# Reordering the first window's second product of an mLSTM cell with a GELU block: who copies columns, when weights are converted, and what a load queues behind

## The chip, the cores and the metric

The kernel runs on one core of a Trainium2 chip. The metric is the device time of one execution in microseconds (us). The program uses five engines, each with an instruction stream of its own: TensorE (PE in the profile; its weight loads are shown apart as PEld), VectorE (DVE), ScalarE (ACT), GpSimd (POOL) and SyncE (SP), which in this kernel issues every DMA transfer. [...] The kernel is written under a manual schedule: on each engine the instructions run in the order in which the program emits them, so moving a call in the source moves its instructions in the stream of each engine it uses.

## The reference

An mLSTM cell (4 batches, 8 heads, 768 steps, head size 40) feeds a two-layer block (3072 tokens, 320 to 2048 to 320) with the quick GELU between.

```python
for t in range(S):                                  # per batch and head
    m_new = max(f[t] + m, i[t])
    C = exp(f[t] + m - m_new) * C + exp(i[t] - m_new) * outer(v[t], k[t])
    n = exp(f[t] + m - m_new) * n + exp(i[t] - m_new) * k[t]
    y[t] = sigmoid(o[t]) * (C @ q[t]) / max(abs(n @ q[t]), 1)
    m = m_new
x = y as (3072, 320)
h = x @ w_in                                        # the first product
out = (h * sigmoid(1.702 * h)) @ w_out              # the second product
```

## The kernel before

The 768 steps are cut into six windows of 128 (w = 0 to 5). Inside a window the recurrence is written as a masked attention (scores, weights, values) plus a term from the carried state. Each window then goes through the first product (`up`, TensorE, with a GELU on ScalarE) and the second (`down` in window 0, `down_fast`, a form with fewer multiplications, in the others). While TensorE does the second product of window w, the attention of window w+1 is slipped in between its blocks. Window 0 is special in two ways: its attention stands ahead of everything, and the 20 pieces of the two weight matrices arrive as 64-bit numbers in this window and are turned into fp32 by ScalarE and VectorE (`convert`), just ahead of the blocks that use them.

Loads. Every one goes out on SP, in program order. `load_blocks` brings k and q of the next window in 32-column blocks, in 32 small transfers, so that VectorE can transpose them (`transposes`); the buffers `k_bl` and `q_bl` exist once. `fetch` brings one piece of weights; pieces 10 to 15 take the six buffers of one pool, and pieces 16 to 19 take them over when the pieces before have been converted.

```python
    def load_blocks(w, which=slice(0, 2)):
        both = (k_bl, k), (q_bl, q)
        for dst, src in both[which] if isinstance(which, slice) else both[which:which + 1]:
            for two in range(2):
                for d in range(0, D, 32):
                    n = min(32, D - d)
                    r = two * 64 + d
                    for g in range(L // 32):
                        t = w * L + g * 32
                        nc.sync.dma_start(
                            out=dst[r:r + 32, :, g, 0:n],
                            in_=src[:, two:H:2, t:t + 32, d:d + n].rearrange("b j s d -> s (b j) d"))
...
    def fetch(n):
        pool = gp if 6 <= n < 10 else sp
        bits[n] = pool.tile([128, 512, 2], U32, tag="g", name="bits")
        for r, c, src in pieces[n][1]:
            dst = bits[n][r, c].rearrange("p a two -> p (a two)")
            if len(src.shape) == 3:
                dst = dst.rearrange("p (j m) -> p j m", j=src.shape[1])
            nc.sync.dma_start(out=dst, in_=src)
...
    def convert(n, engines="AV"):
        lo, hi, dst = bits[n][:, :, 0], bits[n][:, :, 1], pieces[n][0]
        dst_u = dst.bitcast(U32)
        if "A" in engines:
            A.activation(out=dst, in_=hi.bitcast(FP), func=AF.Abs)
            A.activation(out=lo, in_=lo, func=AF.Copy, scale=2.0 ** -29)
        if "V" not in engines:
            return
        V.tensor_scalar(out=dst, in0=dst, scalar1=HI_MIN, scalar2=HI_MAX, op0=OP.max, op1=OP.min)
        V.tensor_scalar(out=dst_u, in0=dst_u, scalar1=3, scalar2=0x3FFFFFFF, op0=OP.logical_shift_left,
                        op1=OP.bitwise_and)
        V.scalar_tensor_tensor(out=dst_u, in0=hi, scalar=0xC0000000, in1=dst_u, op0=OP.bitwise_and,
                               op1=OP.bitwise_or)
        V.tensor_tensor(out=dst_u, in0=dst_u, in1=lo, op=OP.add)
```

The columns of the gates (a transpose on TensorE, evicted to `cols`), the weights of later windows (an exponential for each of 8 heads, then a causal mask on GpSimd), and the first lines of scores and values:

```python
        c = cols[w] = gate.tile([L, 3 * BH + BH // 2], FP, name="cols")
        V.tensor_copy(out=c[:, 0:BH], in_=pt[:, 0:BH])
        A.activation(out=c[:, BH:3 * BH], in_=pt[:, BH:3 * BH], func=AF.Exp, scale=-1.0)
        if w in dec:
            A.activation(out=c[:, 3 * BH:n], in_=pt[:, 3 * BH:n], func=AF.Exp)
...
    def weights(w, b):                    # the branch of w > 0
            x = wt[w, b].rearrange("s p i t -> s (p i) t")
            for h in range(H):
                A.activation(out=x[:, h, :], in_=x[:, h, :], func=AF.Exp, scale=-1.0,
                             bias=cols[w][:, b * H + h:b * H + h + 1])
        x = wt[w, b].rearrange("s p i t -> s (p i) t")
        G.affine_select(out=x, in_=x, compare_op=OP.is_ge, fill=0.0, base=0, pattern=[[0, H], [1, L]],
                        channel_multiplier=-1)
        if w and b == 0:
            A.activation(out=eo[w], in_=eo[w], func=AF.Tanh, scale=0.5)


        pw = [ps_a.tile([L, NP, L], FP, tag="a", name="p_s") for _ in range(2)]
        for p in range(NP):
            for i in range(2):
                r = slice(i * 64, i * 64 + D)
                T.matmul(pw[i][:, p, :], kT[w, b][r, p, :], qT[w, b][r, p, :], start=True, stop=True)
        for i in range(2):
            V.tensor_tensor(out=wt[w, b][:, :, i, :], in0=pw[i], in1=wt[w, b][:, :, i, :], op=OP.mult)


    def values(w, b):
        ...   # 32 matmuls of wt and v_st into p_o, 16 of qT and state into p_i, then 7 operations on DVE that make y
```

The attention of a batch b runs through four stages, each a step after the one before; a step is called after a block of the second product named in `stops`:

```python
    def attention(w):
        steps = [[(columns, w)]]
        for s in range(B + 3):
            step = []
            for lag, f in ((3, seam), (2, values), (1, scores), (0, weights)):
                if 0 <= s - lag < B:
                    step.append((f, w, s - lag))
            steps.append(step)
        return steps
```

The main loop:

```python
    beside = {0: ((5,), range(10, 16)), 1: ((6, 7, 8), ()), 2: ((9, 10, 11), (16, 17)), 3: ((12, 13, 14), (18, 19)),
              4: ((15, 16), ()), 9: ((17,), ()), 12: ((18,), ()), 14: ((19,), ())}

    def weights_in(n):
        done, ahead = beside.get(n, ((), ()))
        for p in done:
            convert(p)
        for p in ahead:
            fetch(p)

    for w in range(NW):
        more = w + 1 < NW
        for j in range(NF // 2):
            if j % 2 == 0:
                if w == 0 and j == 0:
                    up(w, j, (lambda: values(0, 2), lambda: values(0, 3),
                              lambda: (seam(0, 2), seam(0, 3), convert(3), convert(4))))
                    weights_in(0)
                else:
                    if w == 0:
                        weights_in(j // 2)
                    up(w, j)
            if j == 0 and more:
                load(w + 1, "o")
            if w == 0 and j == 0:
                gates(1)
                load_blocks(1, 0)
                spread(1)
            if w == 1 and j == 1:
                weight_sums()
            if more:
                if w and j == 0:
                    gates(w + 1)
                if j == 4:
                    load(w + 1, "v")
                if w and j == 4:
                    spread(w + 1)
                if j == 4:
                    load(w + 1, "k")
                if j < B:
                    carry(w, j)
                if w == 0 and j == 0:
                    G.memset(q_bl, 0.0)
                    load_blocks(1, 1)
                if 4 <= j < 6 if w else j == 7:
                    first = 2 * j - 8 if w else 0
                    transposes(w + 1, first)
                    transposes(w + 1, first + 1)
            if w and j >= 4:
                hidden_sums(w, (j - 4,), False)
                if j % 2:
                    hidden_sums(w, (j - 5, j - 4), True)
        side = attention(w + 1) if more else []
        if w == 0:

            blocks = [(lambda b=b, n=n: down(w, b, n)) for ns in ((0, 1), (2,), (3,)) for b in range(B) for n in ns]
            stops = (0, 1, 4, 7, 9, 11, 13, 15)
        else:
            blocks = down_fast(w, 0) + down_fast(w, 1)
            stops = (0, 1, 2, 4, 6, 8, 10, 12)
        for i, block in enumerate(blocks):
            if w == 0:
                weights_in(4 + i)
                if i in (6, 9):
                    transposes(1, i // 3)
            if w + 2 < NW and i == (0 if w else 9):
                load_gates(w + 2)
                load_blocks(w + 2)
            block()
            if i in stops and side:
                run(side.pop(0))
```

`down(w, b, n)` is 8 matmul instructions over four of the sixteen row groups of w_out (n = 0 to 3); with n = 3 the sum is copied out on VectorE and stored. The 1280 columns of one n are 2.5 pieces of 512: pieces 10 to 14 serve n = 0 and 1, pieces 15 to 17 serve n = 2, and 17 to 19 serve n = 3.

Of the kernel before, what the change touches and what calls it, by code (L numbers as in the profile page):

```python
# [34 lines left out]
def kernel(  # L35
# [14 lines left out]
    BH = B * H  # L50
    DM = H * D
    DFF = moe_w_in.shape[1]
    NW = S // L
# [21 lines left out]
    V, A, G, T = nc.vector, nc.scalar, nc.gpsimd, nc.tensor  # L75
# [20 lines left out]
    def load(w, what, bs=slice(0, B)):  # L96
        hs = slice(bs.start * H, bs.stop * H)
        for c in what:
            if c == "o" and w not in eo:
                eo[w] = ld.tile([L, BH, D], FP, tag="eo", bufs=1, name="eo")  # L100
            dst, src = {"k": (k_st, k), "q": (q_st, q), "v": (v_st, v), "o": (eo.get(w), o_gate)}[c]
            nc.sync.dma_start(out=dst[:, hs, 0:D],
                              in_=src[bs, :, w * L:(w + 1) * L, :].rearrange("b h s d -> s (b h) d"))
# [13 lines that stand above are left out]
# [60 lines left out]
    def keep_busy(n):  # L177
        for _ in range(n):
            T.matmul(p_idle, idle, idle.unsqueeze(1).to_broadcast([128, 4, 128]), start=True, stop=True)
# [35 lines left out]
# [15 lines that stand above are left out]
# [46 lines left out]
    def columns(w):  # L276
        pt = ps_a.tile([L, 3 * BH + BH // 2], FP, tag="a", name="p_cols")
        T.transpose(pt[:, 0:3 * BH], stacked[w], ident[0:3 * BH, 0:3 * BH])
        n = 3 * BH
        if w in dec:  # L280
            n += BH // 2
            T.matmul(pt[:, 3 * BH:n], half.rearrange("p a b -> p (a b)"), dec[w], start=True, stop=True)
        c = cols[w] = gate.tile([L, 3 * BH + BH // 2], FP, name="cols")
        V.tensor_copy(out=c[:, 0:BH], in_=pt[:, 0:BH])
        A.activation(out=c[:, BH:3 * BH], in_=pt[:, BH:3 * BH], func=AF.Exp, scale=-1.0)
        if w in dec:
            A.activation(out=c[:, 3 * BH:n], in_=pt[:, 3 * BH:n], func=AF.Exp)


    def transposes(w, b):  # L290
        for bl, st, dst, name in ((k_bl, k_st, kT, "kT"), (q_bl, q_st, qT, "qT")):
            dst[w, b] = work.tile([128, NP, L], FP, tag=name, bufs=4, name=name)
            if w:
                V.transpose(out=dst[w, b].rearrange("p j t -> p (j t)"),
                            in_=bl[:, b * NP:(b + 1) * NP].rearrange("p j g c -> p (j g c)"))
                continue
            pt = ps_a.tile([128, NP, L], FP, tag="a", name="p_t")
            for p in range(NP):
                h = b * H + 2 * p
                T.transpose(pt[:, p, :], st[:, h:h + 2, :].rearrange("p a b -> p (a b)"), ident)  # L300
            if b == 0:
                keep_busy(1)
            A.copy(out=dst[w, b], in_=pt)

    def spread(w):

        for b in range(B):
            x = wt[w, b] = work.tile([L, NP, 2, L], FP, tag="wt", bufs=4, name="wt")
            nc.sync.dma_start(out=x.rearrange("s p i t -> s (p i) t"),
                              in_=m_row[w][b * H:(b + 1) * H, :].unsqueeze(0).to_broadcast([L, H, L]))  # L310
# [63 lines left out]
    def seam(w, b):  # L374
        if b == 0:
            xT[w] = work.tile([128, 3, B, L], FP, tag="xT", bufs=1, name="xT")
        px = ps_a.tile([128, 3, L], FP, tag="a", name="p_x")
        for c in range(3):
            T.transpose(px[:, c, :], ys[w, b][:, c * 128:(c + 1) * 128], ident)  # L379
        A.copy(out=xT[w][:, :, b, :], in_=px)  # L380
# [162 lines left out]
    def run(calls):  # L543
        for f, *args in calls:
            f(*args)


    def gate_out(b):
# [31 lines left out]
    convert(2)  # L580
    scores(0, 3)
    columns(0)
    gate_out(2)
    gate_out(3)


    beside = {0: ((5,), range(10, 16)), 1: ((6, 7, 8), ()), 2: ((9, 10, 11), (16, 17)), 3: ((12, 13, 14), (18, 19)),
              4: ((15, 16), ()), 9: ((17,), ()), 12: ((18,), ()), 14: ((19,), ())}

    def weights_in(n):  # L590
        done, ahead = beside.get(n, ((), ()))
# [26 lines that stand above are left out]
                if w and j == 0:  # L618
                    gates(w + 1)
                if j == 4:  # L620
                    load(w + 1, "v")
                if w and j == 4:
                    spread(w + 1)
                if j == 4:
                    load(w + 1, "k")
                if j < B:
                    carry(w, j)
                if w == 0 and j == 0:
                    G.memset(q_bl, 0.0)
                    load_blocks(1, 1)  # L630
                if 4 <= j < 6 if w else j == 7:
                    first = 2 * j - 8 if w else 0
                    transposes(w + 1, first)
                    transposes(w + 1, first + 1)
            if w and j >= 4:
                hidden_sums(w, (j - 4,), False)
                if j % 2:
                    hidden_sums(w, (j - 5, j - 4), True)
        side = attention(w + 1) if more else []
        if w == 0:  # L640

            blocks = [(lambda b=b, n=n: down(w, b, n)) for ns in ((0, 1), (2,), (3,)) for b in range(B) for n in ns]
            stops = (0, 1, 4, 7, 9, 11, 13, 15)
        else:
            blocks = down_fast(w, 0) + down_fast(w, 1)
            stops = (0, 1, 2, 4, 6, 8, 10, 12)
        for i, block in enumerate(blocks):
            if w == 0:
                weights_in(4 + i)
                if i in (6, 9):  # L650
                    transposes(1, i // 3)
            if w + 2 < NW and i == (0 if w else 9):
                load_gates(w + 2)
                load_blocks(w + 2)
            block()
            if i in stops and side:
                run(side.pop(0))


# [28 lines left out]
```

## Time and profile before

| | |
|---|---|
| median of 3 runs | 522.97 us (522.74 to 523.1) |
| the profiled execution | span 519.6 us |
| TensorE busy | 507.5 us, 98% |
| VectorE busy | 268.8 us, 52% |
| ScalarE busy | 168.2 us, 32% |
| GpSimd busy | 71.2 us, 14% |
| 16 DMA engines, loads and stores | 44.21 MB, 45.4% of their time |
| window 0: first product | 29 to 68 us |
| window 0: second product, with the attention of window 1 | 68 to 120 us |
| windows 1 to 5 | 120 to 520 us |

The profile gives each engine's busy time, a strip of its business over the span, the chain of work that ended last, groups of instructions, and who waited for whom. L12 is line 12 of the kernel. "SPq L114" is the issuing of a transfer of line 114 on SP. In a list of waits the engine and line that waited stand ahead of the arrow, and what released it stands behind; then come the total in us, the times, and the longest.

### The profile page before, as it was taken

How to read it: one execution, taken by the hardware profiler on the slowest of the kernel's cores; microseconds unless marked ns; L12 is line 12 of the kernel's file. 1: busy time of each engine (PE TensorE's matmuls, PEld its weight loads, DVE VectorE, ACT ScalarE, POOL GpSimd, SP SyncE). 2: the span in 40 equal slices, each digit the busy share in tenths (PEclk: the TensorE clock that was granted, in tenths of full speed). 3: DMA queues.
4: the chain of work that ended last, by engine and by line, in shares of the span. 5: the costliest groups of instructions: out<-in, count | busy, mean ns of one | idle time of the engine just before them, and what ended most of it. 6: DMA issues, size and time to landing. Idle time of an engine off the chain costs nothing.

```text
span 519.6 us, 9543 instructions
## 1 busy us (share of the span) xinstructions
PE 507.5 (98%) x3838; PEld 351.1 (68%) x3838; DVE 268.8 (52%) x603; ACT 168.2 (32%) x367; POOL 71.2 (14%) x104
## 2 busy tenths in 40 slices
PE   7899999999999999999999999999999999999997
PEld 4774366674437998446999444999643899744797
DVE  6779955972774464156444226565227455203511
ACT  5557617502214510321720222630222450032100
POOL 7231001112500212200212200120220021000000
PEclk9999999999999999999999999999999999999999
DMA  9999689166596102596200395500475000000000
GB/s 148 169 315 286 128 169 204 37 75 117 96 194 76 31 1 48 85 212 75 30 26 14 66 253 61 55 28 1 78 175 89 0 28 1 26 0 0 2 26 25
DMA packets 175692, 44.81 MB, mean 86 GB/s; under 512 B 164352, under 2 KB 170528, under 8 KB 175648
## 3 DMA queue, kind: packets, MB, share of 16 engines
q1 hardware_dynamic: 175648, 44.21, 45.4%
q8 instruction: 30, 0.49, 0.4%
q14 instruction: 14, 0.11, 0.1%
HBM read 40.17 MB, written 4.01 MB: 85 GB/s over the span
## 4 chain that ended last, share of the span: by engine, by line
PE 82%; SPq 5%; DVE 4%; ACT 4%; issue 1%; POOL 1%; DMA 1%; DVEq 0%; POOLq 0%
PE p_out L511 30%; PE p_h L417 28%; PE p_h L423 8%; PE p_o L350 5%; SPq L114 4%; PE p_s L339 4%; PE p_out L457 3%; PE p_i L356 2%; PE p_x L379 1%; DMA v_st<-in_v_dram 1%; PE p_c L391 1%; ACT wt L326 1%; ACT bits L221 1%; ACT g L428 1%; ACT w_in_sb L220 0%
## 5 line engine op out<-in xcount | busy, mean ns | idle before, releaser
L417 PE MATMUL p_h<-xT,w_in_sb 128*128 128x512 f32 (+1 forms) x400 | 175.6, 585 | 1.1 <-ACT xT L380 1.1
L417 PEld LDWEIGHTS p_h<-xT,w_in_sb 128*128 128x128 f32 x400 | 72.7, 190 | 90.3 <-issue 86.9
L428 ACT ACTIVATE g<-p_h 128x512 f32<-128x512 f32 x96 | 54.5, 596 | 132.4 <-PE p_h L423 72.3
L511 PE MATMUL p_out<-w_out_sb,g 128*128 128x160 f32 x480 | 71.3, 302 | 0.0
L511 PEld LDWEIGHTS p_out<-w_out_sb,g 128*128 128x128 f32 x480 | 66.8, 190 | 3.7 <-issue 2.4
L516 DVE TENSOR_TENSOR o_sb<-o_sb,p_out 128x160 f32<-128x160 f32 x70 | 21.4, 318 | 65.2 <-PE p_out L511 65.0
L329 POOL TENSOR_SCALAR_AFFINE_SELECT wt<-wt 128x1024 f32<-128x1024 f32 x24 | 26.6, 1110 | 193.8 <-ACT wt L326 190.4
L380 ACT COPY xT<-p_x 128x384 f32<-128x384 f32 x24 | 11.5, 480 | 117.9 <-PE p_x L379 117.8
L423 PE MATMUL p_h<-xT,w_in_x 64*128 64x512 f32 (+1 forms) x200 | 48.7, 599 | 0.9 <-ACT g L428 0.7
L326 ACT ACTIVATE wt<-wt,cols 128x128 f32<-128x128 f32 x160 | 48.4, 393 | 0.0
L511 PE MATMUL p_out<-t,s 128*128 128x160 f32 x320 | 47.5, 301 | 0.0
L511 PEld LDWEIGHTS p_out<-t,s 128*128 128x128 f32 x320 | 44.3, 190 | 0.6
L495 DVE TENSOR_TENSOR s<-g 128x512 f32<-128x512 f32 x20 | 13.8, 692 | 54.0 <-ACT g L428 53.6
L341 DVE TENSOR_TENSOR wt<-p_s,wt 128x512 f32<-128x512 f32 x48 | 30.8, 683 | 17.7 <-POOL wt L329 17.7
L400 DVE TENSOR_TENSOR state<-p_c,state 40x164 f32<-40x164 f32 x32 | 10.4, 326 | 55.6 <-PE p_c L391 55.2
L423 PEld LDWEIGHTS p_h<-xT,w_in_x 64*128 64x128 f32 x200 | 17.4, 186 | 30.3 <-issue 26.9
L457 PE MATMUL p_out<-w_out_sb,g 128*128 128x320 f32 x128 | 36.4, 438 | 0.0
L457 PEld LDWEIGHTS p_out<-w_out_sb,g 128*128 128x128 f32 x128 | 23.7, 190 | 10.4 <-issue 0.5
L350 PE MATMUL p_o<-v_st,wt 128*64 128x41 f32 x768 | 27.6, 231 | 3.0 <-DVE wt L341 2.6
L350 PEld LDWEIGHTS p_o<-v_st,wt 128*64 128x64 f32 x768 | 24.6, 137 | 8.2 <-issue 4.3
L339 PE MATMUL p_s<-qT,kT 40*128 40x128 f32 x384 | 27.9, 285 | 0.4 <-DVE wt L341 0.4
L339 PEld LDWEIGHTS p_s<-qT,kT 40*128 40x128 f32 x384 | 23.3, 187 | 3.9 <-issue 1.1
(114 smaller groups left out, 506.7 us busy)
## 6 DMA issues: line engine op xcount, KB each, us to landing
wt<-m_row SPq DMA_DIRECT2D x20, 512.0 KB, 6.4
bits<-in_moe_w_in_dram SPq DMA_DIRECT2D x8, 512.0 KB, 5.7
out_dram<-o_sb SPq DMA_DIRECT2D x24, 160.0 KB, 1.8
eo<-in_o_gate_dram SPq DMA_DIRECT2D x5, 640.0 KB, 5.6
v_st<-in_v_dram SPq DMA_DIRECT2D x5, 640.0 KB, 5.7
k_st<-in_k_dram SPq DMA_DIRECT2D x5, 640.0 KB, 8.1
bits<-in_moe_w_out_dram SPq DMA_DIRECT2D x8, 320.0 KB, 4.2
k_bl<-in_k_dram SPq DMA_DIRECT2D x40, 64.0 KB, 2.6
```

What stands on the lines that cost most here:

```text
L114: nc.sync.dma_start(out=dst[r:r + 32, :, g, 0:n], in_=src[:, two:H:2, t:t + 32, d:d + n].rearrange("b j s d -> s (b j) d"))
L326: A.activation(out=x[:, h, :], in_=x[:, h, :], func=AF.Exp, scale=-1.0, bias=cols[w][:, b * H + h:b * H + h + 1])
L329: G.affine_select(out=x, in_=x, compare_op=OP.is_ge, fill=0.0, base=0, pattern=[[0, H], [1, L]], channel_multiplier=-1)
L339: T.matmul(pw[i][:, p, :], kT[w, b][r, p, :], qT[w, b][r, p, :], start=True, stop=True)
L341: V.tensor_tensor(out=wt[w, b][:, :, i, :], in0=pw[i], in1=wt[w, b][:, :, i, :], op=OP.mult)
L350: T.matmul(po[t, h, :], wt[w, b][:, p, i, t], v_st[:, b * H + h, :], start=True, stop=True)
L417: T.matmul(ph[j][i][:, ts], w_in_sb[:, c, f * 128:(f + 1) * 128], x[:, c, ts], start=(first and c == 0), stop=(not first and c == 1))
L423: T.matmul(ph[j][i][:, ts], w_in_x[r, j, :], x[r, 2, ts], start=first, stop=not first)
L428: A.activation(out=g[:, i, :], in_=ph[j][i], func=AF.Gelu_apprx_sigmoid)
L457: T.matmul(po, gs[w, f // 2][:, f % 2, b * L:(b + 1) * L], w_out_sb[:, f, :], start=(f == 0), stop=(f == NF - 1))
L511: T.matmul(po, a(f), b[:, f, :], start=(f == 0), stop=(f == NH - 1))
L516: V.tensor_tensor(out=dst, in0=x, in1=po, op=OP.add)
```

## The change

Except for the first point, which holds in every window, it touches the second product of window 0 and what window 0 loads for windows 1 and 2.

- The copy of 32 columns of `cols` goes from VectorE to ScalarE, which does the exponentials beside it.
- The conversion of piece 16 moves one block later, as does that of piece 17.
- The transposes of window 1 leave the end of the first product: batches 0 and 1 go to just ahead of block 2 of the second product, batch 2 from block 6 to block 8, batch 3 from block 9 to block 10.
- The step with the scores of batch 0 goes from after block 4 to after block 5.
- On SP, the fetches of pieces 16 and 17 come ahead of the 16 loads of q for window 1, and those of 18 and 19 come ahead of the load of k.
- The gate and block loads of window 2 go from block 9 of the second product to behind its four stores.

Its purpose is that the exponentials of window 1 do not stand behind a conversion whose weights have not landed, and that stores do not stand behind loads.

```diff
--- before.py
+++ after.py
@@ -281,7 +281,7 @@
             n += BH // 2
             T.matmul(pt[:, 3 * BH:n], half.rearrange("p a b -> p (a b)"), dec[w], start=True, stop=True)
         c = cols[w] = gate.tile([L, 3 * BH + BH // 2], FP, name="cols")
-        V.tensor_copy(out=c[:, 0:BH], in_=pt[:, 0:BH])
+        A.copy(out=c[:, 0:BH], in_=pt[:, 0:BH])
         A.activation(out=c[:, BH:3 * BH], in_=pt[:, BH:3 * BH], func=AF.Exp, scale=-1.0)
         if w in dec:
             A.activation(out=c[:, 3 * BH:n], in_=pt[:, 3 * BH:n], func=AF.Exp)
@@ -585,7 +585,7 @@
 
 
     beside = {0: ((5,), range(10, 16)), 1: ((6, 7, 8), ()), 2: ((9, 10, 11), (16, 17)), 3: ((12, 13, 14), (18, 19)),
-              4: ((15, 16), ()), 9: ((17,), ()), 12: ((18,), ()), 14: ((19,), ())}
+              4: ((15,), ()), 5: ((16,), ()), 10: ((17,), ()), 12: ((18,), ()), 14: ((19,), ())}
 
     def weights_in(n):
         done, ahead = beside.get(n, ((), ()))
@@ -618,20 +618,20 @@
                 if w and j == 0:
                     gates(w + 1)
                 if j == 4:
+                    if w == 0:
+                        load_blocks(1, 1)
                     load(w + 1, "v")
-                if w and j == 4:
-                    spread(w + 1)
-                if j == 4:
+                    if w:
+                        spread(w + 1)
+                if j == (4 if w else 6):
                     load(w + 1, "k")
                 if j < B:
                     carry(w, j)
                 if w == 0 and j == 0:
                     G.memset(q_bl, 0.0)
-                    load_blocks(1, 1)
-                if 4 <= j < 6 if w else j == 7:
-                    first = 2 * j - 8 if w else 0
-                    transposes(w + 1, first)
-                    transposes(w + 1, first + 1)
+                if w and 4 <= j < 6:
+                    transposes(w + 1, 2 * j - 8)
+                    transposes(w + 1, 2 * j - 7)
             if w and j >= 4:
                 hidden_sums(w, (j - 4,), False)
                 if j % 2:
@@ -640,21 +640,24 @@
         if w == 0:
 
             blocks = [(lambda b=b, n=n: down(w, b, n)) for ns in ((0, 1), (2,), (3,)) for b in range(B) for n in ns]
-            stops = (0, 1, 4, 7, 9, 11, 13, 15)
+            stops = (0, 1, 5, 7, 9, 11, 13, 15)
         else:
             blocks = down_fast(w, 0) + down_fast(w, 1)
             stops = (0, 1, 2, 4, 6, 8, 10, 12)
         for i, block in enumerate(blocks):
             if w == 0:
                 weights_in(4 + i)
-                if i in (6, 9):
-                    transposes(1, i // 3)
-            if w + 2 < NW and i == (0 if w else 9):
+                for b in {2: (0, 1), 8: (2,), 10: (3,)}.get(i, ()):
+                    transposes(1, b)
+            elif w + 2 < NW and i == 0:
                 load_gates(w + 2)
                 load_blocks(w + 2)
             block()
             if i in stops and side:
                 run(side.pop(0))
+        if w == 0:
+            load_gates(2)
+            load_blocks(2)
 
 
 # ---- launch: one core; inputs and outputs as the reference has them ----
```

## The prediction

> **What bounds the kernel now.** I read the page first, for the engine that sets the time.
>
> ```profile
> PE 507.5 (98%) x3838; PEld 351.1 (68%) x3838; DVE 268.8 (52%) x603; ACT 168.2 (32%) x367; POOL 71.2 (14%) x104
> ...
> PE 82%; SPq 5%; DVE 4%; ACT 4%; issue 1%; POOL 1%; DMA 1%; DVEq 0%; POOLq 0%
> ```
>
> TensorE is busy for 507.5 of 519.6 us and carries 82% of the chain that ended last. The change takes no work from TensorE, so it can win only idle time of TensorE: 12 us in all. Next, busy time by stretch, to see where those 12 us lie (length, PE, PEld, DVE, ACT, POOL, clock, DMA share, GB/s).
>
> ```profile
> 0.00:20.00 20.00, 15.52 (x176) 10.47 (x176) 14.03 (x37) 9.49 (x18) 10.71 (x23) 1.00 1.11 170
> 20.00:40.00 20.00, 19.03 (x227) 15.21 (x225) 16.11 (x35) 12.64 (x24) 6.35 (x8) 1.00 0.98 260
> 40.00:60.00 20.00, 20.00 (x95) 8.50 (x89) 18.41 (x41) 12.70 (x24) 1.90 (x2) 1.00 0.88 193
> 60.00:80.00 20.00, 20.00 (x72) 11.41 (x72) 13.37 (x25) 8.10 (x15) 0.00 (x0) 1.00 0.83 195
> 80.00:90.00 10.00, 8.79 (x76) 6.30 (x76) 4.61 (x9) 7.48 (x21) 1.11 (x2) 1.00 1.38 183
> 90.00:100.00 10.00, 8.86 (x101) 6.38 (x97) 8.90 (x19) 6.78 (x20) 2.35 (x3) 1.00 0.17 53
> ...
> 160.00:204.00 44.00, 44.00 (x495) 42.09 (x494) 22.51 (x58) 14.60 (x41) 7.99 (x12) 1.00 0.19 29
> ```
>
> From 40 to 80 us TensorE is full, and the later windows are full too (44.00 of 44). The 4.5 us of the first 20 are the start, which the change does not touch. What it can reach is 1.21 + 1.14 us between 80 and 100. The timeline of TensorE there gives each gap in brackets, with what ended it.
>
> ```profile
> 80.71 6.73 PE L457 MATMUL p_out<-w_out_sb,g 128*128 128x320 f32 x24
> 88.36 0.32 PE L350 MATMUL p_o<-v_st,wt 128*64 128x41 f32 x4 [0.93 <-DVE wt L341]
> 88.96 1.02 PE L350 MATMUL p_o<-v_st,wt 128*64 128x41 f32 x28 [0.28 <-DVE wt L341]
> ...
> 97.17 0.54 PE L379 MATMUL p_x<-ident,y 128*128 128x128 f32 x3 [0.79 <-DVE y L370]
> ...
> 98.37 1.02 PE L350 MATMUL p_o<-v_st,wt 128*64 128x41 f32 x28 [0.28 <-ACT xT L380]
> ```
>
> The four gaps add up to 0.93 + 0.28 + 0.79 + 0.28 = 2.28 us. Why are wt (the masked weights of batch 0 of window 1) and y late? The list of waits between 68 and 121 us answers, each line with the total, the times and the longest.
>
> ```profile
> ACT w_out_sb L220 <- DMA bits<-in_moe_w_out_dram: 8.6, 1, 8.6
> DVE qT L294 <- DMA bits<-in_moe_w_out_dram: 5.6, 1, 5.6
> DVE wt L341 <- POOL wt L329: 3.9, 1, 3.9
> ...
> ACT cols L285 <- DVE cols L284: 2.5, 1, 2.5
> ```
>
> ScalarE stood 8.6 us at the conversion of piece 16, whose data had not come. VectorE stood 5.6 us ahead of a transpose of q (the transfer named is the last one to end; the one meant is q_bl, whose 16 issues ran to 74.6), then did pieces 15 and 16, and came to the copy of the columns at 83.57. So the exponentials of batch 0 ran at 83.98 instead of behind the columns, which TensorE had made by 70.9; the mask came at 86.49, the product with the scores at 87.61, and TensorE had been waiting since 87.44. Behind all of it is SP's order: 16 issues of q_bl from 61.88 for 12.70 us, and only then, at 74.67, the fetch of piece 16.
>
> **What the Trainium skill says.** "PSUM — Partial Sum Buffer", section "Engine vs sequencer instructions": the queues of ScalarE and VectorE are strict FIFO. The trace agrees: the exponentials, whose input was there at 70.9, stood behind a conversion until 79.98 and then behind VectorE's copy. "ScalarE: Activation LUTs", section "Table sets: the hidden batching unit": cheap functions (copy and abs are among those it lists) are in every set, and exp and tanh share one. The trace agrees: between 80 and 120 us ScalarE does exp, tanh, abs and copy after one table load at 79.99 of 1.28 us. So a copy on ScalarE costs no further load. "Perfetto Trace Analysis", section "DMA Instruction — HWDGE (DVE, Sync)": the slice of an issue is the making of descriptors, not the movement of data. It agrees: v_st took 0.38 us to issue and 7.4 to land, so I add a landing time to every issue below.
>
> **The change part by part.** I place the streams of the changed kernel by durations of this trace.
>
> SP. The spread of the weights ends at 61.8 as before. Piece 16 can be fetched at once (its buffer came free with piece 10, at 61.2) and piece 17 at 63.6, when VectorE ends piece 11. Five issues at 0.43 us take SP to 64.6. Then 16 issues of q_bl at 0.53: before, two of them stalled for 2.26 and 2.69 us instead of 0.49, and with 1 MB more ahead of them I expect as much again, so 64.6 + 8.5 + 4 = 77, with the last landed about 2.5 us later, at 79.5. v_st goes out at 77.5 and lands 7.4 later, at 85.
>
> ScalarE. Conversion of piece 15 to 70.1; copy of the columns at 70.95 (0.2), table load 1.28, two exponentials 0.3: 72.8. Piece 16, landed by 70: two operations, 1.2 us, to 74.0. The 8 exponentials of batch 0, 2.43 us, to 76.4, tanh 1.26, batch 1 to 80. The mask of batch 0 ends at 77.5, where it ended at 87.58.
>
> VectorE. Pieces 14 and 15 without the wait for q, to 72.9; piece 16 at 74.0 + 2.4 = 76.4; transposes of batches 0 and 1 when q lands: 79.5 + 4 x 0.63 = 82.
>
> TensorE. Block 0 at 68.15, columns to 70.8, then five blocks (1 to 5) at 2.24 us (8.88 us for the 32 matmuls of four is 2.22): 82. Scores of batch 0, 1.1 us, to 83.1: kT and qT of batch 0 were there at 80.8. Blocks 6 and 7 to 87.6, while VectorE multiplies scores by weights (two of 0.68, 84.5). Values of batch 0 at 87.6 find wt and v_st: the gaps of 0.93 and 0.28 go. Values and scores take 2.8, to 90.4. Block 8 needs piece 17, converted by VectorE from 84.5 to 86.9: that also takes away a hidden 0.3 (the 16 matmuls at 91.59 took 4.79 us, those at 101.00 4.57, and a weight load in between waited for L229). y of batch 0 is done at 92, seam after block 9 at 94.9: the gaps of 0.79 and 0.28 go. Carried on in the same way, pieces 18 (landed near 86, converted by 96) and 19 and the last two pairs of transposes stay ahead of the blocks by 1 us or more.
>
> The sum: 2.28 + 0.3 = 2.6 us less, and 0.1 for VectorE's copy (0.18) gone from the crowded end of the first attention near 30 us; minus an allowance of 0.3 for one new small wait where my margins are about 1 us (transposes of q against scores at 82, and kT of batch 3). Net -2.4 us.
>
> Not on the path: the copy in later windows (0.18 on an engine that is half idle, while TensorE is full); the stores of window 0, which before stood behind 32 loads until 118.72 and held VectorE 3.6 us (it delayed nothing that TensorE waited for). The 0.57 us at 120 stays, since the last seam has no block behind it.
>
> **The rivals.** First, the late loads of window 2 become a wait. They leave the stretch from 88 to 118 and are issued after the last store, at about 117.5: gates to 118.5, 32 issues at 0.53 to 136, landed by 138.5. VectorE uses them at 143.0 less the 2.4 gained, so 2 us of margin, and behind the transposes VectorE idled 2.18 us before the next GELU. The gates of window 2 are wanted at 120 and land near 124, but VectorE then idled 7.19 us before the first state. The row of maxima, o, and the spread behind the blocks would go out about 137 to 144 and land by 151, wanted at 162. I hold this free; if wrong, it costs 1 to 3 us and the change is worth nothing, about 522 to 523.5. Second, q lands later than I think, because the fetches take its place: then the scores at 82 wait, by 1 or 2 us, and the values behind them follow: 521.5 to 522. For it: SP stalled for 5 us in just this stretch. Against: the bytes are the same, only their order differs. Third, hidden anyway: TensorE's gaps are only moved from one wait to the next, as VectorE is the second busiest engine there (8.90 of 10 us between 90 and 100). Against it: it loses its 5.6 us wait at 71, and that work moves earlier. This would give 522.5.
>
> **Range and chances.** 522.97 - 2.4 = 520.6. If all idle time of the stretch went and nothing else came, 520.3; a further wait that goes, at 125 us (0.68 behind a GELU, whose cause the trace does not settle), makes 519.6. The low end is 519.4, the high end 522.4, where the second rival takes most of the gain. 2% is 10.5 us, nearly all of TensorE's idle time in the whole kernel, most of it in stretches that stay as they are: faster by 2% has 0.01. Slower by 2% would need a stall of 10 us in a later window, 0.01. Within 2%: 0.98.
>
> **What would show it.** Right: no wait of 8.6 us at L220 and none of VectorE for q; the first exponentials of window 1 at 74 us and not 84; no bracket of over 0.2 us on TensorE from 80 to 100; the first product of window 1 starting at 118 and not 120.5; the same distances from there to the end. Wrong: a gap ahead of the scores at 82, v_st landing after 87.6, or a gap on TensorE between 140 and 165, where window 2's loads would show.

## The result, and the profile after

The changed kernel takes 516.42 us (median of 4 executions, 516.32 to 518.0), the kernel before 522.86 beside it: a ratio of 0.9892, 95% interval 0.9862 to 0.9922. That is 6.4 us less, where 2.4 were predicted, and outside the predicted range. A second set of runs gave 516.41 against 522.47, ratio 0.9877 (0.9857 to 0.9898).

The page of the changed kernel, busy times and the chain that ended last:

```profile
PE 507.3 (98%) x3838; PEld 352.0 (68%) x3838; DVE 270.3 (52%) x597; ACT 169.1 (33%) x373; POOL 71.0 (14%) x104
...
PE 94%; DVE 2%; POOL 1%; ACT 1%; issue 1%; DVEq 0%; POOLq 0%
```

TensorE's share of the chain rose from 82 to 94%, and the issuing of loads, 5% before, is gone from it. The stretches of the changed kernel (length, PE, PEld, DVE, ACT, POOL, clock, DMA share, GB/s):

```profile
0.00:20.00 20.00, 15.59 (x152) 10.54 (x152) 15.85 (x37) 8.91 (x16) 10.39 (x22) 0.95 1.11 168
20.00:40.00 20.00, 18.98 (x212) 15.32 (x211) 14.58 (x32) 11.84 (x25) 6.61 (x8) 0.96 0.97 244
...
80.00:90.00 10.00, 10.00 (x85) 7.10 (x85) 5.33 (x9) 5.76 (x16) 1.09 (x1) 1.00 1.01 198
90.00:100.00 10.00, 9.98 (x116) 7.84 (x112) 8.82 (x21) 3.59 (x11) 1.27 (x2) 1.00 0.48 46
```

The two stretches from 80 to 100 us, 8.79 and 8.86 before, are full. The seventh column is TensorE's granted clock: it was 0.95 and 0.96 in the first 40 us of this execution, which is why everything after them stands 1.6 us late in it. In the second set a profiled execution of the same kernel had full clock and a span of 514.7 us; the lines and distances below are from that one.

TensorE there, with its waits in brackets:

```profile
82.64 4.57 PE L457 MATMUL p_out<-w_out_sb,g 128*128 128x320 f32 x16
87.14 1.13 PE L350 MATMUL p_o<-v_st,wt 128*64 128x41 f32 x32
...
94.30 0.49 PE L379 MATMUL p_x<-ident,y 128*128 128x128 f32 x3
...
117.10 3.70 PE L417 MATMUL p_h<-xT,w_in_sb 128*128 128x512 f32 x8 [0.57 <-ACT xT L380]
120.73 1.99 PE L423 MATMUL p_h<-xT,w_in_x 64*128 64x512 f32 x8
```

The four brackets of the kernel before are gone; that of 0.57 stays. ScalarE and VectorE show why:

```profile
73.53 2.43 ACT L326 ACTIVATE wt<-wt,cols 128x128 f32<-128x128 f32 x8
...
78.70 0.71 DVE L294 STREAM_TRANSPOSE qT<-q_bl 128x512 f32<-128x512 f32 x1 [2.55 <-DMA q_bl<-in_q_dram]
```

The first exponentials of window 1 run at 73.53 and not at 83.98. VectorE still stands 2.55 us at q, but the transposed q is there 2.1 us before TensorE uses it at 81.55.

The last line of TensorE's list is the surprise. In the kernel before, the same eight matmuls of L423 were two groups:

```profile
124.16 1.13 PE L423 MATMUL p_h<-xT,w_in_x 64*128 64x512 f32 x4
125.97 1.61 PE L423 MATMUL p_h<-xT,w_in_x 64*128 64x512 f32 x4 [0.68 <-ACT g L428]
127.51 3.70 PE L417 MATMUL p_h<-xT,w_in_sb 128*128 128x512 f32 x8
```

From 124.16 to the next L417 they took 3.35 us instead of 1.92 (120.73 to 122.65). Both profiled executions had full clock. The starts of TensorE's stretches (first block of window 0's second product, first and second product of window 1) are 68.15, 120.53 and 159.88 in the kernel before, and 67.93, 117.10 and 155.02 in the changed one. By the distances between them, the gain lies so:

| stretch | before | changed | difference | predicted |
|---|---|---|---|---|
| start to first block of window 0's second product | 68.15 | 67.93 | -0.2 | -0.1 |
| that block to window 1's first product | 52.38 | 49.17 | -3.2 | -2.6, +0.3 |
| window 1's first product to its second | 39.35 | 37.92 | -1.4 | 0 |
| from there to the end | 359.72 | 359.68 | 0.0 | 0 |
| span | 519.6 | 514.7 | -4.9 | -2.4 |

The rest of the 6.4 us is in the kernel before: its profiled execution took 521.27 us, 1.6 less than the median of the first set.

### The profile page after: what moved, and what is told of

The parts are those of the page before. It is cut to its first block, busy times and chain, and to the rows that moved or that the text cites. A ratio compares the mean times of both kernels' runs of the same rounds, so it can differ in the third digit from the quotient of the medians.

```text
span 516.3 us, 9527 instructions
## 1 busy us (share of the span) xinstructions
PE 507.3 (98%) x3838; PEld 352.0 (68%) x3838; DVE 270.3 (52%) x597; ACT 169.1 (33%) x373; POOL 71.0 (14%) x104
## 4 chain that ended last, share of the span: by engine, by line
PE 94%; DVE 2%; POOL 1%; ACT 1%; issue 1%; DVEq 0%; POOLq 0%
PE p_h L417 33%; PE p_out L511 30%; PE p_h L423 9%; PE p_out L457 7%; PE p_o L350 5%; PE p_s L339 4%; PE p_i L356 2%; PE p_c L391 1%; PE p_x L379 1%; DVE wt L341 0%; ACT xT L380 0%; DVE pick L192 0%; POOL k_bl L555 0%; PE p_cols L282 0%; POOL state L554 0%
## 5 line engine op out<-in xcount | busy, mean ns | idle before, releaser
L417 PE MATMUL p_h<-xT,w_in_sb 128*128 128x512 f32 (+1 forms) x400 | 175.6, 585 | 1.2 <-ACT xT L380 1.2
L417 PEld LDWEIGHTS p_h<-xT,w_in_sb 128*128 128x128 f32 x400 | 72.7, 190 | 90.4 <-issue 86.9
L423 PE MATMUL p_h<-xT,w_in_x 64*128 64x512 f32 (+1 forms) x200 | 48.0, 598 | 0.2 <-DVE w_in_x L229 0.2
L423 PEld LDWEIGHTS p_h<-xT,w_in_x 64*128 64x128 f32 x200 | 17.2, 186 | 29.0 <-issue 27.4
L372 POOL COPY y<-y 128x64 f32<-128x64 f32 x24 | 5.7, 236 | 148.2 <-DVE y L370 143.1
```

The costliest lines, as they stand in the source:

```text
L417: T.matmul(ph[j][i][:, ts], w_in_sb[:, c, f * 128:(f + 1) * 128], x[:, c, ts], start=(first and c == 0), stop=(not first and c == 1))
L423: T.matmul(ph[j][i][:, ts], w_in_x[r, j, :], x[r, 2, ts], start=first, stop=not first)
```

## The experiments

Three questions were open: what the 1.4 us in window 1 are, which parts of the change carry the 3.2, and why executions of the kernel before differ by up to 5 us. Runs that stand together in the table shared one chip and the runs of the kernel before. The last two columns take only the executions whose TensorE had full clock throughout (0.999 or more).

| kernel | median us | ratio to before (95%) | at full clock | median of these |
|---|---|---|---|---|
| before | 521.54 | | 27 of 42 | 521.18 |
| stores alone | 519.84 | 0.9962 (0.9941 to 0.9984) | 12 of 14 | 519.57 |
| copy alone | 519.89 | 0.9953 (0.9934 to 0.9973) | 7 of 13 | 518.76 |
| three output buffers | 522.03 | 1.0004 (0.9988 to 1.0020) | 10 of 22 | 520.76 |
| loads back at block 9 | 530.96 | 1.0168 (1.0139 to 1.0198) | 0 of 6 | |
| before | 522.47 | | 5 of 11 | 522.04 |
| changed | 516.41 | 0.9877 (0.9857 to 0.9898) | 6 of 6 | 516.41 |
| copy and stores | 518.14 | 0.9912 (0.9892 to 0.9932) | 5 of 6 | 517.92 |
| changed, copy on VectorE | 517.39 | 0.9901 (0.9877 to 0.9925) | 3 of 6 | 516.62 |
| changed, cut block, idle matmuls | 515.58 | 0.9862 (0.9841 to 0.9882) | 5 of 5 | 515.58 |
| before | 521.87 | | 16 of 26 | 521.50 |
| before, idle matmuls | 521.84 | 1.0001 (0.9982 to 1.0020) | 8 of 14 | 521.45 |
| changed, loads at block 11 | 519.21 | 0.9950 (0.9932 to 0.9968) | 6 of 7 | 519.21 |
| changed, old order on SP | 518.72 | 0.9939 (0.9918 to 0.9960) | 6 of 11 | 517.88 |
| new order on SP alone | 525.32 | 1.0070 (1.0045 to 1.0096) | 0 of 7 | |

**The 1.4 us of window 1: which PSUM buffer a hidden sum gets.** PSUM holds the sums that TensorE writes; a hidden sum is one of the first product's. TensorE waited there for the GELU of the sums just made. The buffers that the built programs assign say why: the pool has four, here named 4 to 7. "Pair" is the two sums of one pair of row groups in window 1's first product.

```
                        outputs of       pair 0   pair 1   pair 2   pair 3
                        batches 0 to 3
before                  7 5 6 4          7 5      7 5      7 5      6 4
changed                 7 5 6 4          7 5      6 4      7 5      6 4
stores alone            7 5 6 4          7 5      6 4      7 5      6 4
three output buffers    7 5 6 4          7 5      6 7      5 6      7 4
loads at block 11       7 5 6 4          7 5      7 5      7 5      7 5
```

In the kernel before, pair 1 shares the buffers of pair 0, so its matmuls must wait until two GELUs have read them, although buffers 6 and 4 had been copied out by 122.25, ahead of the 124.16 at which pair 1 starts:

```profile
121.36 0.89 DVE L461 COPY o_sb<-p_out 128x320 f32<-128x320 f32 x2 [3.62 <-DMA out_dram<-o_sb]
```

The order of loads and stores on SP was the only thing changed in the first experiment:

```diff
-            if w + 2 < NW and i == (0 if w else 9):
+            if w and w + 2 < NW and i == 0:
                 load_gates(w + 2)
                 load_blocks(w + 2)
 ...
+        if w == 0:
+            load_gates(2)
+            load_blocks(2)
```

> The kernel before with one part of the change: the gate and block loads of window 2 go behind the four stores. Nothing else moves, so the gaps of TensorE in the second product of window 0 (0.93, 0.28, 0.79, 0.28 us) stay. PSUM-buffer theory: in the kernel before, the second pair of hidden sums of window 1 was given the two buffers of the first pair, since when the program was built two output sums counted as still held behind the late stores; TensorE therefore waited for two GELUs. With the stores first, the program gives it the buffers of the output sums. The stretch from the first product of window 1 to its second product becomes 38.1 us instead of 39.5, and the whole 1.4 us shorter. Rival (the late stores and VectorE's wait of 3.6 us were off the path, as the prediction held): 0.

The stretch took 37.91 us and not 39.35, and the time fell by 1.6 (519.57 against 521.18). That moving loads alone changes the assignment is shown. That the pool takes an output's buffer as held while its copy waits for a store behind 32 loads is the reading that fits all five rows; it is not shown, as no run tests the pool itself. Next, the late stores with a third buffer for the outputs:

```diff
-    op = ctx.enter_context(tc.tile_pool(name="op", bufs=2))
+    op = ctx.enter_context(tc.tile_pool(name="op", bufs=3))
```

> The kernel before with three buffers for the outputs instead of two, loads and stores in the old order. In the program built so, the second pair of hidden sums of window 1 gets one buffer of an output sum and one of the first pair. PSUM-buffer theory: its first half starts at once, its second waits for one GELU, near 0.35 us instead of 1.43: about 1.1 us less than before. Rival (it is the store order that costs): 0.

The stretch took 38.85: 0.5 less, not 1.1. One shared buffer costs 0.94 of the 1.43: the second sum of pair 1 now waits for the first GELU, which ends some 0.5 us before the second. The median did not move, since only 10 of 22 of its executions were at full clock, where the kernel before had 27 of 42; the medians at full clock differ by 0.4. Then the changed kernel with late stores again:

```diff
-            elif w + 2 < NW and i == 0:
+            if w + 2 < NW and i == (0 if w else 11):
 ...
-        if w == 0:
-            load_gates(2)
-            load_blocks(2)
```

> The changed kernel with the loads of window 2 ahead of block 11: behind the last transposes this time, but ahead of the four stores. As the program is built, the second and the fourth hidden sums' pairs of window 1 (and the third behind the second) all share two PSUM buffers. PSUM-buffer theory: two waits for GELUs of 1.4 us each and one of 0.6 to 0.8 between them; the first product of window 1 grows from 38.1 to 41 to 42 us, the whole by 3 to 4 us against the changed kernel; the second product of window 0 stays at 49.2. Rival (loads ahead of stores are free): 0.

TensorE in that kernel:

```profile
120.66 1.13 PE L423 MATMUL p_h<-xT,w_in_x 64*128 64x512 f32 x4
122.47 1.61 PE L423 MATMUL p_h<-xT,w_in_x 64*128 64x512 f32 x4 [0.68 <-ACT g L428]
...
132.02 1.13 PE L423 MATMUL p_h<-xT,w_in_x 64*128 64x512 f32 x4
133.82 1.61 PE L423 MATMUL p_h<-xT,w_in_x 64*128 64x512 f32 x4 [0.68 <-ACT g L428]
```

Two waits: the stretch is 40.78, 2.86 more than 37.92 and twice 1.43, with the second product at 49.17 as in the changed kernel. They are those of pairs 1 and 3. Pair 2 shares the buffers of pair 1 as well, in this kernel and in the kernel before, but does not wait: the matmuls of the carry (L391, 127.64 to 128.38) stand between the two, and the first GELU of pair 1 has ended at 127.49 by then. So the wait expected between the two did not come. An earlier form of this test (the loads at block 9, not 11) put them ahead of the last transposes:

> The changed kernel with the loads of window 2 put back to block 9, ahead of the stores. PSUM-buffer theory: the buffers of the built program stay apart here (the second pair has the output sums' buffers), so it costs at most what VectorE's wait for the stores adds on TensorE: the second pair then waits until the copies are out, near 122 us in the kernel before, while it starts at 125; so 0, at most 0.3 us. Rival (stores behind loads cost in themselves, whatever the buffers): 1.4 us longer than the changed kernel.

Its expectation overlooked that the change had moved these transposes behind block 9. They therefore took the columns of window 2, so this kernel computes something else, and VectorE stood until those loads had landed:

```profile
116.08 2.08 PE L339 MATMUL p_s<-qT,kT 40*128 40x128 f32 x16 [11.97 <-DVE qT L294]
```

It says nothing on the two theories, though its first product took 37.92 us with the buffers apart. It does show that window 2's loads must stay behind the last transposes of window 1.

**The 3.2 us of the second product.** First one line of the change in the kernel before:

```diff
-        V.tensor_copy(out=c[:, 0:BH], in_=pt[:, 0:BH])
+        A.copy(out=c[:, 0:BH], in_=pt[:, 0:BH])
```

> The kernel before with one line changed: ScalarE copies the columns. Chain theory (the exponentials of batch 0 stood first behind the conversion of piece 16 until 79.98, and then 2.5 us behind VectorE's copy): they start near 81.4 instead of 83.98, the masked weights are there near 85.2, TensorE does not wait at 87.4, and the first of the late steps, 4.15 us from the end of block 7 to block 8, falls to 2.75: 1.4 us less, with 0.1 to 0.2 more from the same copy near 30 us; 1.2 to 1.6 in all. Rival (it takes the order of loads on SP as well, for the conversion of piece 16 is what is late): 0 to 0.2.

It saved 2.4 us at full clock (518.76 against 521.18), more than expected. ScalarE in this kernel, whose profiled execution comes to the second product 3.7 us late, as its clock was at half from 18.5 to 28.7 us:

```profile
81.83 0.69 ACT L220 ACTIVATE w_out_sb<-bits 128x512 f32<-128x512 f32 x1 [8.06 <-DMA bits<-in_moe_w_out_dram]
82.42 0.67 ACT L221 ACTIVATE bits<-bits 128x512 uint32<-128x512 uint32 x1
82.99 0.17 ACT L284 COPY cols<-p_cols 128x32 f32<-128x32 f32 x1
...
84.66 2.44 ACT L326 ACTIVATE wt<-wt,cols 128x128 f32<-128x128 f32 x8
```

ScalarE still waits for piece 16 (8.06 us), but its exponentials no longer wait for VectorE, which converts pieces 15 and 16 first: they start 2.8 us after the wait's end, not 5.3 (83.98 less 78.71). That took all the waits of the stretch in this execution: 49.37 us. Both parts together:

> The kernel before with two parts of the change only: the copy of the columns on ScalarE, and the loads of window 2 behind the stores. The orders of fetches, conversions, transposes and scores stay old. Theory that these two carry it: the copy gives 3.0 to 3.2 in the second product of window 0 (49.4 us from its first block to the next first product, as in the run with the copy alone), the stores 1.4; 4.4 to 4.7 below before at full clock, within 0.4 us of the changed kernel. Rival (the parts overlap, or the reordering carries a part of its own): 1 us or more short of it.

517.92 at full clock, 4.1 below the kernel before and 1.5 above the changed kernel: the two parts add up (2.4 and 1.6 alone), but the reordering carries a part of its own, as the rival had it. In the profiled execution piece 16 landed later (ScalarE waited 9.1 us for it) and a part of the waits was back, the stretch 50.42:

```profile
96.55 0.54 PE L379 MATMUL p_x<-ident,y 128*128 128x128 f32 x3 [0.53 <-DVE y L370]
...
97.75 1.02 PE L350 MATMUL p_o<-v_st,wt 128*64 128x41 f32 x28 [0.28 <-DVE wt L341]
```

Now the reverse, the changed kernel with this line undone:

> The changed kernel with the copy of the columns back on VectorE. If the reordering does the same work as the copy (VectorE no longer stands at q ahead of the columns): the columns are copied at 73 us, behind the conversion of piece 15, and the exponentials start 1 us later at most: 0 to 0.3 us above the changed kernel, most of it near 30 us. Rival (only the copy's engine matters): 3 us above it.

516.62 at full clock, 0.2 above, with 49.16 us for the stretch: with the conversions and transposes reordered, VectorE copies the columns at 72.93, ahead of its wait for q. Copy and reordering cure the same wait. The copy without the reordering stays 1.5 us short, the reordering without the copy 0.2. The order of loads is no part that can be left out or taken alone. Without it:

```diff
                 if j == 4:
-                    if w == 0:
-                        load_blocks(1, 1)
                     load(w + 1, "v")
 ...
-                if j == (4 if w else 6):
+                if j == 4:
                     load(w + 1, "k")
 ...
                     G.memset(q_bl, 0.0)
+                    load_blocks(1, 1)
```

> The changed kernel with the old order of loads on SP for window 1: q ahead of the fetches of pieces 16 and 17, k at its old place. Copy, conversions, transposes and scores are as changed. Theory that the orders belong together: ScalarE waits for piece 16 until 78.7 ahead of the exponentials, VectorE converts it until 82.4 and then transposes, so the scores of batch 0, wanted at 82, wait until 83.7: 1.5 to 2 us above the changed kernel, perhaps with a fall of the clock behind it. Rival (the copy and the stores alone carry the gain): 0.

Its TensorE waits ahead of the scores, for q as VectorE transposes it:

```profile
83.82 1.16 PE L339 MATMUL p_s<-qT,kT 40*128 40x128 f32 x16 [2.26 <-DVE qT L294]
```

517.88 at full clock is 1.5 above the changed kernel, which was not run in this third group. The spread at full clock tells the same: 516.88 to 518.72 here, 517.74 to 518.36 with copy and stores, but 516.38 to 516.45 in the changed kernel and 516.55 to 516.63 with its copy back on VectorE. So in these runs the time no longer hangs on when a transfer lands only where both orders are changed. And the same order of loads by itself, in the kernel before:

> The kernel before with the new order of loads on SP alone: pieces 16 and 17 ahead of q. Theory: ScalarE no longer waits for piece 16, but VectorE, whose order is old, stands at the transposes until q lands near 80, 3 us later than before; then conversions of 15 and 16, the columns at 86 to 87, exponentials behind them; TensorE waits near 88 us for 3 us more than before: 3 us slower or more, and most executions below full clock. Rival (the fetches ahead are a gain by themselves): 1 us faster.

525.32 us, 3.5 above the kernel before; all seven executions were below full clock, so a part of it is the clock. Its list of waits:

```profile
ACT cols L285 <- DVE cols L284: 13.0, 1, 13.0
DVE qT L294 <- DMA q_bl<-in_q_dram: 7.4, 1, 7.4
...
PEld p_o L350 <- DVE wt L341: 3.5, 2, 3.1
```

Piece 16 no longer holds ScalarE, but VectorE stands at q (7.4 us), and the exponentials stand at VectorE's copy for 13.0. The wait went from one engine to the next.

**Why executions of the kernel before differ.** The 1.6 us between its profiled execution and the median of the first set have no single cause. At full clock its 48 executions in the table took 519.83 to 522.47 us, and the profiled one, 521.27, lies amid them. Four kernels with its order of loads and engines up to 88 us show how the waits differ. ScalarE's wait for piece 16, and TensorE's two waits for the masked weights together, are 8.6 and 0.6 us with the stores alone, 8.6 and 1.2 in the kernel before, 9.0 and 1.7 with idle matmuls, 9.9 and 2.2 with three output buffers. These waits change with the landing of transfers: VectorE's wait for q in the four is 5.0, 5.6, 6.1 and 6.5. Besides, the clock falls in two executions of five, which lifts the median by 0.4 us above that at full clock in each group of the table. The clocks of the first set's executions are not on record, so its 1.6 us can't be divided between the two. TensorE's clock in the kernel with three output buffers, whose waits of 1.88 and 0.28 us ended at 89.32 and 89.92 (length, PE, clock, DMA share, GB/s):

```profile
88.00:90.00 2.00, 0.40 (x6) 1.00 1.37 170
90.00:92.00 2.00, 2.00 (x48) 0.86 1.04 358
92.00:94.00 2.00, 2.00 (x17) 0.50 0.27 88
94.00:96.00 2.00, 2.00 (x5) 0.50 0.00 0
96.00:98.00 2.00, 2.00 (x5) 0.50 0.00 0
98.00:100.00 2.00, 2.00 (x9) 0.93 0.00 0
```

For 6.8 us the clock was at half. A fall of 3.4 us in the changed kernel's first profile follows a wait of 1.52 us that ended at 16.8. To tell the two places apart, the kernel before got six idle matmuls (their sums are used by nobody) in the early wait alone:

```diff
     transposes(0, 2)
+    keep_busy(6)
     values(0, 0)
```

> The kernel before with six idle matmuls in TensorE's wait of 1.5 us near 15 us, and nothing else. Theory of two places where the clock falls (after the wait at 15 us, and after the wait at 88 us, whose length differs from run to run with the landing of piece 16 and of q): executions below full clock stay, a fifth or more of them at 0.993 or lower, and where the profiled one is among them, half clock shows between 88 and 100 us; times at full clock still spread over 2 us. Rival (all low clocks come from the wait at 15 us): every execution at full clock, near 521.

Six of 14 executions were still below full clock, and the profiled one was at half clock from 89.6 to 93.0 us, behind a wait of 1.41 that ended at 88.76: the clock falls behind the late wait too, when the early one is filled. The times at full clock spread over 1.2 us, less than expected. Then the changed kernel as it is:

> The changed kernel itself, unaltered, beside the runs of the kernel before. At a full TensorE clock it stands 4.7 us below the kernel before at full clock (516.4 against 521.1). Theory of the second cost (a wait of TensorE of 0.9 to 1.9 us near 88 us lets its clock fall to half for some 7 us, as was seen after the wait of 1.88 us in the run with three output buffers): no execution of the changed kernel shows half clock after 80 us, so fewer of them are below full clock than of the kernel before, and the gap of the medians is 5 to 6 us. Rival (the clock falls at random in both alike): the same share below full clock, gap 4.7.

All six at full clock, within 0.07 us of each other; the earlier set had one of four below it (0.997, behind the early wait). The kernel before had 48 of 79 at full clock. The difference of the medians is 6.1 here and 5.6 at full clock, not 4.7, as the kernel before was 0.9 slower at full clock in this group than in the first. That the changed kernel falls less often is likely, but not shown: with its copy back on VectorE, and no late wait either, three of six executions were below full clock.

**A version that beats both.** The 0.57 us ahead of window 1's first product can be covered by half a block. `down` takes the row groups it is to do, and the last block is cut; the idle matmuls are added as above.

```diff
-    def down(w, b, n):
+    def down(w, b, n, fs=range(4)):
 ...
-        for f in range(n * 4, n * 4 + 4):
+        for f in (n * 4 + k for k in fs):
 ...
+            blocks[15:] = [lambda: down(w, 3, 3, (0, 1)), lambda: down(w, 3, 3, (2, 3))]
```

> The changed kernel with two additions. The last block of window 0's second product is cut in two, and the last seam goes between the halves: TensorE's wait of 0.57 us for the last copy, ahead of the first product of window 1, goes; 0.5 to 0.6 us less. And six idle matmuls fill the 1.5 us that TensorE waits near 15 us: if that wait is what lets the clock fall between 17 and 26 us (costing 1.6 us in the profiled execution of the changed kernel), no execution falls below full clock, and all lie near 515.8. Rival: the clock falls as often as before, and only the 0.5 us remain.

```profile
114.94 0.49 PE L379 MATMUL p_x<-ident,y 128*128 128x128 f32 x3
115.27 1.24 PE L457 MATMUL p_out<-w_out_sb,g 128*128 128x320 f32 x4
116.35 3.60 PE L417 MATMUL p_h<-xT,w_in_sb 128*128 128x512 f32 x8
```

515.58 us, 0.8 below the changed kernel and 0.9862 of the kernel before. The half block stands between the last seam (the step that turns y into the input of the first product) and the first product, no bracket is left, and the second product takes 48.43 us: 0.74 less. All five executions lay within 0.04 us; but the changed kernel also fell only once in ten executions, so whether the idle matmuls do anything is open.

## Why the prediction was wrong

The mechanism predicted, the exponentials freed and TensorE's gaps between 80 and 100 us closed, is what happened. What failed is one step, that the late stores cost nothing, and the size of other terms. Of the 4.0 us between 2.4 predicted and 6.4 measured, 1.4 are the late stores, 0.6 the gaps, 0.3 the allowance, 0.1 the copy near 30 us, and 1.6 the time from which the sum was taken.

- **"It delayed nothing that TensorE waited for"** is the step that failed, on the late stores. They delayed nothing while the kernel ran, but moving the loads changed which PSUM buffers the program was built with: 1.4 us. The bracket of 0.68 at 125 us was seen, and put down as unsettled; it was in the low end of the range and not in the sum, and its cost, 1.43 us, was twice what the bracket showed.
- **2.28 + 0.3 for the four gaps** was 3.2. From the start of one group of blocks to the next (80.71 to 91.59 before, with 24 matmuls; 82.64 to 89.89 in the changed kernel, with 16), less their matmuls at 0.28, the attention between took 4.2 us and now takes 2.8: 1.4, where the brackets show 1.21. For the next group (91.59 to 101.00, now 89.89 to 97.56) it is 1.7, where I had 1.4. A matmul of 128x320 is listed at 438 ns, but the next starts 0.27 to 0.28 us after it on average, so the last one ahead of a gap hides some 0.16 us of it as busy time.
- **The allowance of 0.3 for a new small wait** was not needed: scores at 81.55 found q transposed at 79.4 (predicted 80.8), values at 87.14 found v_st landed at 82.9 (predicted 85), y was done at 91.5 (predicted 92).
- **522.97 less the gaps of one profile** mixed two executions. The profiled one took 521.27, and its gaps have to be taken from that time. What made three other executions of that first set 522.74 to 523.1 is open (waits that were longer, or a clock that fell).
- **The parts.** The 0.1 near 30 us was 0.2. The start of the exponentials, predicted at 74 us, was 73.53. Window 2's loads, the first rival, went out from 117.15 to 135.8; VectorE waited 2.45 us for the gates, and TensorE for none of them, as predicted. The second rival, q landing late, was real only without the new orders of the engines. The third did not occur. One sign named for being right, no wait of VectorE for q, did not appear: it waited 2.55 us. The sign contradicted the prediction's own streams, which had VectorE ready at 76.4 and q landing at 79.5.

## What to carry to other kernels

An engine in order makes everything behind a stalled instruction late: look for the instruction that stands first in line, and expect several moves to cure the same wait, so that their gains do not add up. Where buffers are assigned when a program is built, moving a load or a store can change which buffer a later matmul gets; after any reordering compare what each first write to a buffer waits for. And measure a gap from start to start, over several executions, before taking it as the most that a change can bring. A change that fills a gap may also take away what made executions differ.

## What the runs showed of the hardware

TensorE's clock fell to half in seven of the 14 profiled executions, leaving out the last microseconds of each. The falls begin in a wait of TensorE or up to 2.2 us behind one: one of 1.44 to 1.52 us near 15 us in three, the late ones of 1.41, 1.88 and 2.63 us (idle matmuls, three output buffers, new order on SP alone), and one of 11.97 us (loads back at block 9). They last 3.41 us in four, and 6.83, 10.24 and 17.07 in one each, which are whole multiples of 3.413. But the length of the wait does not decide alone: the early wait, of 1.43 to 1.52 us, stood in 12 of these executions and the clock fell behind it in three, and behind a wait of 2.26 us (old order on SP) it did not fall.

The mean clocks of executions come in steps: 1.000, 0.996, 0.993, 0.990, which is what none, one, two and three stretches of 3.4 us at half clock make of 515 us. In the first group of the table, the medians of the kernel before at these steps were 521.2, 522.2, 523.1 and 524.7 us.

The Trainium skill, "TensorE: Matmul & The Clock Gate", section "What's actually happening", has a free-running window of 3413 ns and two states, half and full, which agrees; but it lets the clock fall after a whole idle window, and here it fell behind waits of about half of one.
